# Sparse attention and gated feed-forward in one kernel: the first unit's prologue in another order, block maxima read from PSUM, block means 128 columns wide

## The chip, the cores and the metric

The kernel runs on one core of a Trainium2 chip. A core has five engines with a queue each: TensorE (PE; its weight loads are listed as PEld), VectorE (DVE), ScalarE (ACT), GpSimd (POOL) and SyncE (SP). Here POOL and SP mostly issue transfers. SBUF is the working memory, PSUM the eight banks that TensorE writes. The metric is the device time of one execution in microseconds.

## The reference

Attention over 4 batches, 8 heads, 768 positions and 64 elements a head, in which a query sees its neighbours within 16 positions and one summary for each block of 32 positions: the maximum of the keys and the mean of the values. Its output is the input of a gated feed-forward layer.

```python
k_sum = k.reshape(B, H, nb, block, D).max(axis=3)       # block 32
v_sum = v.reshape(B, H, nb, block, D).mean(axis=3)
mask_l = np.abs(pos[:, None] - pos[None, :]) < window   # window 16
scores_l = np.where(mask_l, scale * q @ k^T, -1e9)
scores_s = scale * q @ k_sum^T + np.log(block)
a = softmax(concat([scores_l, scores_s]))
x = a @ concat([v, v_sum])                              # 3072 x 512
out = x + sigmoid(x @ w_res) * ((gelu(x @ w_gate) * (x @ w_val)) @ w_out)   # 512 -> 1536 -> 512
```

## The kernel before

Inputs are float32; the transfers of k, q, v and the weights turn them into bf16. The work is cut into eight units of 384 positions, two for each batch. Each unit needs attention for its 384 rows, then 12 column blocks of gate and value products (`fo_step`, 4 + 4 products of 128x384 each), then the products with `w_res` and `w_out`. The attention of unit n+1 is laid between the output products of unit n (`first_out`, `mid_out`). Only unit 0 has nothing before it to hide in: its attention is the prologue, lines 476 to 551.

The schedule is manual: each engine's queue holds its instructions in the order in which the code gives them, and an instruction waits for semaphores of the engines that wrote its inputs or last used its buffer. PSUM has four pools: `ps_mm` (four banks, tag mm), `ps_s` (two banks, for a pair's scores), `ps_o` and `ps_t` (one each).

Heads are handled in four pairs. For a pair of unit 0:

- `turn_pair` (L219) transposes the loaded k or q on TensorE into a PSUM tile `tp`.
- `k_place` copies k from PSUM into `kW` with ScalarE (L251). Then VectorE takes the block maxima (`k_blocks`: reduction L236 into `ks`, copy to each tile of 64 queries L240) and copies the neighbours of each tile of 64 keys (`k_rims`, L244 and L245). So each tile's 128 columns are 64 own keys, 32 neighbours, 24 block maxima and 8 unused. `q_place` copies q (ScalarE, L258).
- `s_step` makes the scores: in unit 0 two mask products (L311) write the additive mask, then 12 products (L318) add the scores. ScalarE takes the exponential (L336, or two halves L333 where the scores lie in two separate banks, `MM2`).
- `vsum_pair` makes the block means of v: 12 accumulating products (L284) of a 64x32 averaging matrix `bmat`, out of partitions 96 to 127 of the PSUM tile, copied into `vblk` (L286).
- `pair_rims` copies neighbours of the v tiles (VectorE, L274 and L271). `av_band` multiplies P with the 96 rows of v (L366), `av_blk` with the 32 rows of block means (L366), and `av_end` divides by the sums (L372, L374).
- `xt_step` transposes the result into `xT` (L379, L381), the operand of the gate and value products `gv_mm` (L394). `gv_end` is GELU on ScalarE (L399) and a product on VectorE (L400).

`keep_warm` (L474) is a filler: products of zeros with 512 columns, whose output nobody reads. The first call has 12 of them, before the first k arrives. POOL's queue issues all loads in a fixed order; eight may be under way, and each further one waits for the transfer eight earlier.

## Time and profile before

| what | us |
|---|---|
| median of 4 runs (lowest to highest) | 264.74 (263.96 to 264.91) |
| the profiled execution | 264.91 |
| its span | 263.1 |
| first k arrives, transposes of k start | 6.44 |
| scores of the first pair | 11.08 |
| first attention product | 15.34 |
| first gate product | 26.03 |
| gate product of column block 2 starts | 31.06 |
| TensorE's granted clock is half | 16.12 to 29.77 |

The span is the part of the execution in which the engines have work; the time also counts what lies around it. All places in time are counted from the start of the span. "Idle before" in a row is the engine's gap ahead of an instruction, with what ended it. The granted clock is 1.00 for full speed. It is shown as 1.00 from the start on, but the first 12 fillers run at half speed: 512 columns each 0.42 us, as against 0.22 later. The first change that the trace records is at 5.88.

### The profile page before, as it was taken

The numbers are of one execution on the slowest core, as the hardware profiler recorded it, in microseconds if no ns is written. First come the engines' busy times: TensorE is split into PE (matmuls) and PEld (weight loads), VectorE is DVE, ScalarE is ACT, GpSimd is POOL, SyncE is SP. The second block draws the span as 40 slices with busy tenths as digits, with TensorE's granted clock in tenths as the row PEclk, the third lists the DMA queues.
The fourth block names the chain that finished last, engine by engine and source line by source line (L and its number), as shares of the span: only waits on it lengthen the run. The fifth ranks groups of instructions, "written<-read, shape, count | busy, mean of one in ns | idle before, by whom it ended". The sixth has DMA issues, their size and how long they took to land.

```text
span 263.1 us, 5837 instructions
## 1 busy us (share of the span) xinstructions
PE 253.9 (97%) x2299; PEld 142.6 (54%) x2322; DVE 161.8 (62%) x368; ACT 127.1 (48%) x213; POOL 97.1 (37%) x128
## 2 busy tenths in 40 slices
PE   7889999999999999999999999999999999999994
PEld 2556555456555456545655555545654565556544
DVE  6784289739856744675947744766858544764424
ACT  6754235836666344933373436624383437443320
POOL 8785443540151695029144683238304000000000
PEclk9975799999999999999999999999999999999999
DMA  5999999994901599939932899949903500140003
GB/s 83 169 184 196 197 206 207 165 124 136 145 7 25 127 166 146 124 97 171 120 78 45 140 181 153 99 115 166 150 7 62 161 0 4 35 145 2 2 0 120
DMA packets 98106, 29.33 MB, mean 112 GB/s; under 512 B 83224, under 2 KB 94944, under 8 KB 97984
## 3 DMA queue, kind: packets, MB, share of 16 engines
q0 software_dynamic: 68352, 14.76, 66.7%
q1 hardware_dynamic: 29728, 14.21, 26.3%
q8 instruction: 18, 0.29, 0.5%
q14 instruction: 8, 0.07, 0.1%
HBM read 29.36 MB, written 6.29 MB: 136 GB/s over the span
## 4 chain that ended last, share of the span: by engine, by line
PE 83%; DMA 6%; DVE 6%; issue 2%; POOL 1%; ACT 0%; POOLq 0%; DVEq 0%
PE vv L394 22%; PE g L394 22%; PE f L442 22%; PE r L432 8%; DMA q_sb<-in_q_dram 4%; PE s L318 3%; PE ao L354 3%; DMA k_sb<-in_k_dram 3%; PE tp L219 1%; PE vs L292 1%; DVE vext L556 1%; DVE P L340 1%; DVE ks L236 1%; PE ao L366 1%; DVE o L451 1%
## 5 line engine op out<-in xcount | busy, mean ns | idle before, releaser
L400 DVE TENSOR_TENSOR gvT<-ge,vv 128x384 bf16<-128x384 f32 x96 | 52.7, 553 | 48.7 <-PE vv L394 44.4
L399 ACT ACTIVATE ge<-g 128x384 f32<-128x384 f32 x96 | 47.0, 491 | 71.0 <-DVE gvT L400 38.9
L394 PE MATMUL vv<-xT,w_val 128*128 128x384 bf16 x384 | 79.6, 328 | 0.6 <-DVE gvT L400 0.5
L394 PE MATMUL g<-xT,w_gate 128*128 128x384 bf16 x384 | 79.8, 329 | 0.1
L442 PE MATMUL f<-w_out,gvT 128*128 128x512 bf16 x262 | 62.7, 379 | 1.5 <-issue 1.1
L394 PEld LDWEIGHTS <-w_gate 128*128 128x128 bf16 x384 | 37.4, 99 | 27.1 <-issue 2.6
L394 PEld LDWEIGHTS <-w_val 128*128 128x128 bf16 x384 | 37.8, 98 | 26.2 <-issue 1.7
L442 PEld LDWEIGHTS <-gvT 128*128 128x128 bf16 x276 | 25.7, 98 | 29.5
L107 POOL DMA_DIRECT2D vext<-in_v_dram x32 | 24.5, 793 | 15.4 <-DMA w_out<-in_moe_w_out_dram 5.1
L435 ACT ACTIVATE th<-r 128x512 f32<-128x512 f32 x24 | 13.5, 607 | 27.9 <-PE r L432 27.9
L448 DVE SCALAR_TENSOR_TENSOR th<-th,f 128x512 f32<-128x512 f32 (+2 forms) x26 | 16.6, 640 | 14.6 <-PE f L442 14.6
L432 PE MATMUL r<-w_res,xT 128*128 128x512 bf16 x88 | 22.7, 380 | 0.4
L340 DVE TENSOR_TENSOR P<-P,maskt 128x768 bf16<-128x768 bf16 x28 | 16.7, 597 | 9.9 <-ACT P L336 5.2
L304 POOL COPY vext<-vsum 32x1536 bf16<-32x1536 bf16 x12 | 17.2, 1463 | 13.7 <-DMA vsum<-vpart 13.5
L451 DVE SCALAR_TENSOR_TENSOR o<-th,xn 128x512 f32<-128x512 f32 (+2 forms) x26 | 18.2, 701 | 0.9
L374 DVE TENSOR_TENSOR xn<-ao,rz 128x384 bf16<-128x384 f32 x32 | 17.8, 558 | 1.1
L336 ACT ACTIVATE P<-s,bias_t 128x768 bf16<-128x768 f32 x17 | 15.3, 902 | 6.2 <-PE s L318 6.0
L236 DVE TENSOR_REDUCE ks<-kW 128x24 bf16<-128x768 bf16 x16 | 15.1, 946 | 1.6 <-ACT kW L251 1.6
L127 POOL DMA_DIRECT2D q_nat<-in_q_dram x18 | 15.8, 901 | 0.8 <-issue 0.7
L333 ACT ACTIVATE P<-s,bias_t 128x384 bf16<-128x384 f32 x30 | 15.7, 579 | 0.8 <-PE s L318 0.8
L432 PEld LDWEIGHTS <-xT 128*128 128x128 bf16 x96 | 8.8, 98 | 9.9
L372 DVE RECIPROCAL rz<-ao 128x6 f32<-128x6 f32 x32 | 6.1, 192 | 11.8 <-PE ao L354 9.8
(86 smaller groups left out, 190.1 us busy)
## 6 DMA issues: line engine op xcount, KB each, us to landing
out_dram<-o SPq DMA_DIRECT2D x23, 256.0 KB, 2.2
vext<-in_v_dram POOLq DMA_DIRECT2D x32, 96.0 KB, 6.9
q_nat<-in_q_dram POOLq DMA_DIRECT2D x18, 128.0 KB, 5.5
w_gate<-in_moe_w_gate_dram POOLq DMA_DIRECT2D x6, 256.0 KB, 9.1
w_val<-in_moe_w_val_dram POOLq DMA_DIRECT2D x6, 256.0 KB, 9.7
w_out<-in_moe_w_out_dram POOLq DMA_DIRECT2D x3, 512.0 KB, 14.1
k_nat<-in_k_dram POOLq DMA_DIRECT2D x16, 96.0 KB, 6.0
vext<-vext SPq DMA_DIRECT2D x6, 144.0 KB, 4.8
```

The source lines that it names most:

```text
L107: nc.gpsimd.dma_start(out=vext[b % 2][0:QT, :, h, 0:D], in_=v[b, h].rearrange("(t p) d -> p t d", p=QT))
L236: nc.vector.tensor_reduce(out=ks.rearrange("d (t n) -> d t n", n=2), in_=kw[:, :, 0:QT].rearrange("d t (n w) -> d t n w", w=BLK), axis=myb ...
L304: eng.tensor_copy(vext[b % 2][96:128, lo:hi, :, 0:D], src)
L340: nc.vector.tensor_mul(Pf, Pf, maskt.unsqueeze(1).to_broadcast([128, 2 * HT, QT]))
L374: nc.vector.tensor_mul(xn, ao[:, :, :, 0:D], rz.to_broadcast([128, NSUB, 2, D]))
L394: nc.tensor.matmul(ps[:, 0:TU], w[:, ko, fo * 128:(fo + 1) * 128], st["xT"][:, ko, :], start=(ko == 0), stop=(ko == KO - 1), skip_group_ch ...
L399: nc.scalar.activation(ge[:], g[:, 0:TU], AF.Gelu)
L400: nc.vector.tensor_mul(gvT[:, fo, :], ge[:], vv[:, 0:TU])
L432: nc.tensor.matmul(r[:], st["xT"][:, ko, ss], w_res[:, ko, :], start=(ko == 0), stop=(ko == KO - 1))
L442: nc.tensor.matmul(st["f", sub][:], gvT[:, fo, ss], w_out[:, fo, :], start=(fo == 0), stop=(fo == FO - 1), skip_group_check=True)
L448: nc.vector.scalar_tensor_tensor(th[:, cs], th[:, cs], 1.0, f[:, 0:n], ALU.add, ALU.mult)
L451: nc.vector.scalar_tensor_tensor(o.rearrange("p (k d) -> p k d", d=128), th[:, cs].rearrange("p (k d) -> p k d", d=128), 0.5, x, ALU.mult, ...
```

## The change

The prologue of unit 0 is written in another order, which moves instructions on TensorE, ScalarE and VectorE. All four transposes of the first half (k and q of pairs 0 and 1) come first. Pair 0 then goes to its scores before the second half of k is transposed, and q of pair 1 is placed after the exponential of pair 0. The mask for later units (`maskt`) is made after the last k. The scores of pairs 1 and 2 come before the first attention product, those of pair 3 behind it, and the means of pairs 1 to 3 between the attention products. The fillers are spread otherwise: after the first 12, five, one, one, one and one become one, two, one, one, one and one, some in another bank. The gate and value products of blocks 0 and 1 change their order among each other.

The block maxima of k, where k was transposed on TensorE (batches 0 and 1), are read from the PSUM tile and not from `kW`. The averaging matrix has three zero slots of 32 columns ahead of it, and each block mean product takes four slots as its weights: 128 columns, of which the last 32 are the former ones. The means of pair 3 are copied by ScalarE and no longer by VectorE. The clearing of `bmat` and `bgrp` moves out of `own_keys`.

```diff
-    bmat = const.tile([QT, NT, 32], BF16, name="bmat")
+    bmat = const.tile([QT, NT + 3, 32], BF16, name="bmat")
...
         def own_keys(m, n):
-            nc.vector.memset(m[:], 0.0)
...
-        own_keys(bmat, NT)
+        nc.vector.memset(bmat[:], 0.0)
+        own_keys(bmat[:, 3:, :], NT)
...
-        def k_blocks(b, hp):
+        def k_blocks(b, hp, tp=None):
...
+            if tp is None:
...
+            else:
+                nc.vector.tensor_reduce(
+                    out=ks[:], in_=tp.rearrange("d j (n w) -> d n w j", w=BLK // PJ),
+                    axis=mybir.AxisListType.XY, op=ALU.max)
             nc.vector.tensor_copy(kw[:, :, BAND:BAND + NB], ks.unsqueeze(1).to_broadcast([128, NT, NB]))
...
-        def k_step(b, hp, pool, tag):
-            k_place(b, hp, turn_pair(k_sb[b], hp, turn_tile(k_sb[b], pool, tag)))
+        def k_turn(b, hp, pool, tag):
+            return turn_pair(k_sb[b], hp, turn_tile(k_sb[b], pool, tag))
...
-            k_blocks(b, hp)
+            k_blocks(b, hp, tp)
...
-        def vsum_pair(hp, pool, tag, copy):
+        def vsum_pair(hp, pool, tag):
...
-                nc.tensor.matmul(vs[96:128, 0:2 * D], bmat[:, t, :], vext[0][0:QT, t, hs, 0:D],
+                nc.tensor.matmul(vs[:, 0:2 * D], bmat[:, t:t + 4, :], vext[0][0:QT, t, hs, 0:D],
                                  start=(t == 0), stop=(t == NT - 1))
-            copy(vblk[96:128, hs, 0:D], vs[96:128, 0:2 * D].rearrange("p (h d) -> p h d", d=D))
+            nc.scalar.copy(vblk[96:128, hs, 0:D], vs[96:128, 0:2 * D].rearrange("p (h d) -> p h d", d=D))
...
-        def keep_warm(n):
-            wp = ps_s.tile([128, 2, 512], F32, tag="s", name="wp")
+        def keep_warm(n, pool=ps_s, tag="s"):
+            wp = pool.tile([128, 2 if pool is ps_s else 1, 512], F32, tag=tag, name="wp")
...
-        mm = (ps_mm, "mm")
+        mm, t_bank, o_bank = (ps_mm, "mm"), (ps_t, "t"), (ps_o, "ao")
         keep_warm(12)
-        k_step(0, 0, *mm)
-        k_step(0, 1, *mm)
-        q_step(0, *mm)
-        q_step(1, *mm)
+        tk = {hp: k_turn(0, hp, *mm) for hp in range(2)}
+        tq = {hp: q_turn(hp, *mm) for hp in range(2)}
+        k_place(0, 0, tk[0])
+        q_place(0, 0, tq[0])
+        k_place(0, 1, tk[1])
         mt = ps_o.tile([128, 128], BF16, tag="ao", name="mt")
         nc.tensor.transpose(mt[:], mneg[:], ident[:])
-        nc.vector.tensor_scalar(out=maskt[:], in0=mt[:, 0:QT], scalar1=-1.0, scalar2=None, op0=ALU.is_ge)
-        keep_warm(5)
-        k_step(0, 2, *mm)
-        k_step(0, 3, *mm)
+        keep_warm(1)
         st = new_unit()
         s_step(0, 0, st)
-        s_step(0, 1, st, MM2)
-        t2 = [q_turn(2, *mm), q_turn(3, *mm)]
-        vsum_pair(0, ps_t, "t", nc.scalar.copy)
-        q_place(0, 2, t2[0])
-        q_place(0, 3, t2[1])
-        keep_warm(1)
-        pair_rims(0)
-        vsum_pair(1, ps_o, "ao", nc.scalar.copy)
+        q_place(0, 1, tq[1])
+        keep_warm(2, *t_bank)
+        for hp in range(2, 4):
+            tk[hp] = k_turn(0, hp, *mm)
+            k_place(0, hp, tk[hp])
+        nc.vector.tensor_scalar(out=maskt[:], in0=mt[:, 0:QT], scalar1=-1.0, scalar2=None, op0=ALU.is_ge)
+        for hp in range(2, 4):
+            tq[hp] = q_turn(hp, *mm)
+            q_place(0, hp, tq[hp])
+        s_step(0, 1, st)
+        keep_warm(1, *t_bank)
+        vsum_pair(0, *t_bank)
+        s_step(0, 2, st, MM2)
...
+        pair_rims(0)
+        av_band(0)
+        s_step(0, 3, st)
         pair_rims(1)
-        av_band(0)
         av_blk(0)
-        s_step(0, 2, st)
+        vsum_pair(1, *o_bank)
+        pair_rims(2)
         av_band(1)
-        s_step(0, 3, st, MM2)
-        pair_rims(2)
         av_blk(1)
-        vsum_pair(2, ps_t, "t", nc.scalar.copy)
+        vsum_pair(2, *t_bank)
         nc.scalar.activation(gate1[:], bias_t[0:1, :], AF.Gelu)
         keep_warm(1)
+        pair_rims(3)
         av_band(2)
-        pair_rims(3)
-        vsum_pair(3, ps_o, "ao", nc.vector.tensor_copy)
...
         av_blk(2)
-        xt_step(0, 0, st, **turn[0])
+        keep_warm(1)
...
+        xt_step(0, 0, st, **t_turn)
+        vsum_pair(3, *o_bank)
         av_band(3)
+        xt_step(0, 1, st, **t_turn)
         keep_warm(1)
         av_blk(3)
-        xt_step(0, 1, st, **turn[1])
-        keep_warm(1)
...
```

The rest of the diff is the new order of the gate and value products of blocks 0 and 1 with the last two transposes between them: g0 (0, 1), transpose 2, g1 (0, 1), g0 (2), g1 (2), transpose 3, v0 (0 to 2), v1 (0 to 2), then the last part of each.

## The prediction

> **What bounds the kernel now.** I read the page first: the span, the engines, and the row of the TensorE clock.

> ```profile
> span 263.1 us, 5837 instructions
> ...
> PE 253.9 (97%) x2299; PEld 142.6 (54%) x2322; DVE 161.8 (62%) x368; ACT 127.1 (48%) x213; POOL 97.1 (37%) x128
> ...
> PEclk9975799999999999999999999999999999999999
> ```

> TensorE is busy 97% of the span, but between slices 2 and 4 its granted clock is not full. I then cut that stretch finer. The columns are: stretch, its length, busy time and instructions of PE, PEld, DVE, ACT, POOL, then granted clock, DMA share, GB/s.

> ```profile
> 5.88:9.29 3.41, 2.97 (x55) 1.59 (x54) 2.01 (x21) 2.27 (x4) 3.14 (x5) 1.00 1.30 189
> 9.29:12.71 3.42, 2.87 (x80) 2.00 (x80) 3.07 (x10) 2.29 (x4) 2.31 (x4) 1.00 2.17 157
> 12.71:16.12 3.41, 2.59 (x50) 1.90 (x48) 3.25 (x11) 2.34 (x7) 3.20 (x5) 1.00 2.21 167
> 16.12:19.53 3.41, 3.41 (x56) 2.02 (x55) 2.54 (x7) 1.66 (x3) 2.85 (x5) 0.50 1.46 197
> 22.95:26.36 3.41, 3.41 (x47) 2.12 (x47) 1.81 (x5) 0.96 (x2) 2.24 (x3) 0.50 1.45 196
> 26.36:29.77 3.41, 3.41 (x16) 1.99 (x15) 0.36 (x1) 0.48 (x1) 1.85 (x3) 0.50 1.45 196
> 29.77:33.19 3.42, 3.33 (x21) 1.87 (x20) 1.57 (x3) 1.36 (x3) 1.61 (x3) 1.00 1.46 200
> ```

> The clock is halved from 16.12 to 29.77, 13.65 us, and TensorE has no idle time in it: this is where the prologue can win. Up to 15.34 other engines set the pace. The timeline of these engines, then of TensorE:

> ```profile
> 10.42 1.50 ACT L251 COPY kW<-tp 128x768 bf16<-128x768 bf16 x2 [1.14 <-PE tp L219]
> 11.25 0.95 DVE L236 TENSOR_REDUCE ks<-kW 128x24 bf16<-128x768 bf16 x1 [0.28 <-ACT kW L251]
> 14.82 0.46 DVE L271 COPY vext<-vext 16x768 bf16<-16x768 bf16 x1
> ```

> ```profile
> 15.34 0.38 PE L366 MATMUL ao<-vext,P 96*64 96x65 bf16 x12 [0.43 <-DVE vext L271]
> ...
> 19.13 1.46 PE L284 MATMUL vs<-vext,bmat 64*32 64x128 bf16 x12
> ...
> 26.03 0.53 PE L394 MATMUL g<-xT,w_gate 128*128 128x384 bf16 x1
> ...
> 31.06 0.81 PE L394 MATMUL g<-xT,w_gate 128*128 128x384 bf16 x4
> ```

> The first attention product waits for the V rims that VectorE ends at 15.29. The chain of waits then names a transfer:

> ```profile
> 19.20 1.40 PE vs L284 x12
> 20.61 0.48 issue
> 21.08 9.96 DMA q_sb<-in_q_dram
> 31.04 0.01 issue
> 31.06 0.81 PE g L394 x4
> ```

> I don't believe it: TensorE has no gap there, and the tile is read only at 42.85. My mark is the start of the third gate product, 31.06; from there on the two kernels run the same order.

> [...] here a window with TensorE busy 2.59 of 3.41 us was followed by the drop, and three with no idle time did not end it[...]. [...] No reduction from PSUM is in this trace.

> **The change part by part**, against the profiled 264.91 us (span 263.1, 1.8 around it; the median of the runs is 264.74, 0.17 less).

> *Block maxima from PSUM.* The built program shows each reduction still waiting for ScalarE's copy of the same pair, so it starts no earlier. 0.946 us now; [...] I take 0. It holds its PSUM bank longer: the q transpose of pair 2 waits for the second reduction, which ends at 10.15, before its own data. The four reductions of batch 1 change too; their banks' next users come a product block (1.3 us) or more later.

> *Block means 128 wide.* Twelve products take 0.84 us at full clock and 1.46 at half (spacing 54 and 107 ns), which is their 128 moving columns. The weight load grows from 56 ns to the 98 of other 128-wide loads; 128-wide ones of half the rows keep up at 12 in 0.35 us (the scores). I take 0, at worst 12 x 44 ns x 4 = 2.1 us if a load no longer overlaps. The gain is that each fills half the array, not an eighth.

> *New order, to the first attention product.* Pair 0 goes first: its copy 7.01-7.82, reduction 7.84-8.79, rims to 9.30, scores to 9.65 (now 11.4), exponential (0.9) to 10.57. It now stands ahead of q 1 (0.44) and of the K copy of pair 2, so that starts at 11.0, not 10.42. Behind it: reduction 11.82-12.77, rims to 13.25, last reduction and rims to 14.75, mask 0.17, V rims of pair 0 (0.83) to 15.85. So the attention product of pair 0 starts 0.5 us LATER, and TensorE, done with the scores of pair 2 by 14.15, idles 1.7 us. For this, scores of pairs 1 and 2 lie before it; ScalarE's row (copies to 12.5, q to 13.4, exponentials 0.9 + 1.05, one means copy) ends at 15.6, and the last exponential at 17.8, not 19.8.

> *From 15.85 on at full clock.* Attention band 0.31, last scores 0.7, rest of pair 0 0.31 (17.15); means 1, 0.68 (17.85); pair 1 with its means copy 0.26 between, 0.65 (18.5); means 2 and a filler (19.4); pair 2, a filler, transpose (20.5); means 3 (21.1). VectorE's V rims and normalizations (0.83 and 0.76 each) end at 20.5 for pair 3, before it. Band 3 (21.4); the second transpose waits for the first's copy out of the same bank, which waits for ScalarE's table load (19.5-21.0): 21.75. Filler, rest of pair 3 (22.25); then 16 gate and value products at 0.163 with two transposes and their copies: 25.6. That is 5.4 us before 31.06. I take off 0.5, about 0.03 for each of some 16 hand-overs between engines (the chain shows 0.02 to 0.05): **-4.9 us**.

> *Moved past queues.* POOL's transfers keep their order and are released by the transfer eight earlier, so they land where they land now. Read from these releases: gate chunk 1 by 21.1 (used 31.06), q half 1 by 32.7 (42.85), w_res 37.9 (46.9), w_out 40.5 to 45.5 (49.4 to 54.6), k of batch 1 49.3 (61.3). The least cover is 9 us; it hides a shift of 5. SP's queue starts later and keeps its order. The changed memset grows from 64x192 to 64x240 words, 0.05 us under the wait for k. Between 31 and 43 VectorE's fill-in work sets the pace now and then (idle before gate products 0.50 at the most); it is the same work and moves with the rest.

> **The clock decides.** I count moving columns times the used share of rows and of weight columns; a full window at 0.163 us per 384 is 8,040. Before the drop (12.71-16.12): 22 means x 16, one filler 512, attention 391, mask product about 400: 1,655, 21%. The window before, which kept the clock: mask 1,536, scores 768, transposes 1,728, means 64: 51%, or 29% without transposes. So the bar is between 21% and 29 or 51. The changed kernel there: 11 means x 64, mask 768, scores 384, two thirds of a band 195: 2,051, 25%. From 16.12 it has 40% and more. That is inside the bracket; I take it as just enough, because the means alone go from 352 to 704 columns. With whole columns counted instead of cells, it is 39% against 29% at the drop.

> **Rivals.** *The same drop.* The 1.7 us of idle time leaves the window too thin, and the clock halves at 16.12 as now. Then TensorE's own work is the bound: at 16.12 the new order still has means 1 (1.40) and the rest of pair 0 (0.52) to do, the old one most of one score block (1.0): 0.9 us more, of which half is run after 29.77 at double speed: +0.45, 265.4.

> *Slower: an earlier drop.* Fillers before 9.29 go from five to one. In 5.88-9.29 I count fillers 1,024, mask 896, transposes 1,728: 45%, as against 58% now; but without transposes 24% against 35%. If transposes don't count and the bar is above 24%, the clock halves at 9.29. The next window's transposes, scores and means at half speed cost 1.35 more; the first gate product starts at 28.4 instead of 26.03. If the window to 29.77 still counts as full, the end is +1.1 us, 266.0; if not, all 16 products run at 0.325 until 33.19: +2.8, 267.7.

> *Part of the gain.* The clock holds at 16.12 but falls for one window later, or wide loads don't overlap: 2 to 3 us lost, 262.5. *It doesn't do what it says*: true of the reductions, above; it costs nothing.

> **How the numbers follow.** Full clock 52% (own range 258.4 to 261.5), part 8%, same drop 23%, earlier drop 17%. The likeliest gives 264.91 - 4.9 = 260.0. The range runs from 258.4 to 266.0, over the two middle cases and the near half of the earlier drop. 0.3% (0.8 us) is about what a measurement can tell. Faster: 52 + 7 = 59%. Within 0.3%: two thirds of the same drop and 1, 16%. Slower: the rest of it and the earlier drop, 25%.

> **What would show it.** Right: clock 1.00 in every window after the first start, scores of pair 0 near 9.3, the first attention product near 15.85, gate products of the third column block near 26, and the shift carried unchanged to the end. Wrong: a clock of 0.50 from about 16 (same drop) or 9.3 (earlier), a K copy of pair 2 that starts before 10.6, means spaced wider than 60 ns, or TensorE waiting for a weight transfer.

## The result, and the profile after

The changed kernel takes 265.27 us (median of 12 runs, 263.94 to 266.19); the kernel before took 264.09 beside it (median of 17 runs, 258.88 to 265.08). The difference of the medians is +1.18 us, 0.4% slower; the prediction was 260.0. The ratio of the comparison is 1.0201, 95% interval 1.0144 to 1.0257, but it sets the mean of all 12 runs against that of before's four fastest alone (258.88, 258.93, 259.46 and 262.75).

That spread belongs to the result. In the profiles, an execution at a mean clock of 0.998 to 1.0 has no half-clock stretch in its course, one at 0.980 (e9) has one of some 10.2 us, one at 0.972 or 0.973 (before, after) has one of 13.65 us: three and four windows of 3.41 us. Over this comparison and those of the experiments, before was under 260 us in 14 of 65 runs. The changed kernel never was: four runs at 0.980 (263.94 to 264.36), eight at 0.972 to 0.974 (264.79 to 266.19). Where before's clocks are listed (48 runs, those beside the experiments), its medians are 259.22 at the full clock (11 runs), 263.47 at 0.980 (21) and 264.84 below 0.975 (16); the changed kernel's are 264.27 and 265.97. So it is 0.8 to 1.1 us slower at a like clock, and none of its runs has the full clock, which one run of before in five has. Twelve runs without one could come by chance, about one time in eighteen; e10 and e14 below, which leave the gap open or fill it with few rows, add eight more without one.

The page of the profile after (265.39 us, the span 1.9 less), its span, engines and granted clock:

```profile
span 263.5 us, 5834 instructions
...
PE 253.5 (96%) x2296; PEld 142.9 (54%) x2320; DVE 159.9 (61%) x367; ACT 127.1 (48%) x213; POOL 96.8 (37%) x128
...
PEclk9985699999999999999999999999999999999999
```

The stretch cut at the steps of the clock (columns as in the prediction: stretch, length, busy time and instructions of PE, PEld, DVE, ACT, POOL, clock, DMA share, GB/s):

```profile
6.93:10.35 3.42, 2.54 (x59) 1.48 (x54) 2.27 (x5) 2.30 (x4) 2.55 (x4) 1.00 1.43 186
10.35:13.76 3.41, 3.35 (x78) 2.41 (x77) 2.27 (x9) 3.41 (x7) 2.85 (x5) 1.00 2.43 158
13.76:17.17 3.41, 1.71 (x52) 1.05 (x50) 2.74 (x9) 1.82 (x5) 3.25 (x5) 1.00 1.81 177
17.17:20.59 3.42, 3.42 (x58) 3.02 (x51) 2.38 (x7) 1.06 (x2) 2.46 (x4) 0.50 1.48 201
20.59:24.00 3.41, 3.41 (x41) 2.17 (x40) 1.42 (x4) 2.23 (x4) 1.66 (x3) 0.50 1.43 192
24.00:27.41 3.41, 3.05 (x40) 2.23 (x40) 0.72 (x2) 0.74 (x2) 2.10 (x3) 0.50 1.45 196
27.41:30.83 3.42, 3.42 (x16) 1.76 (x15) 0.39 (x2) 0.48 (x1) 1.75 (x3) 0.50 1.45 197
30.83:34.24 3.41, 3.32 (x21) 1.92 (x20) 1.73 (x4) 1.59 (x4) 1.57 (x3) 1.00 1.39 202
```

The clock is half for four windows again, from 17.17 to 30.83 (before 16.12 to 29.77). The window that the drop follows has TensorE busy for 1.71 of 3.41 us; before it was 2.59. The timeline of VectorE, then of ScalarE:

```profile
11.93 0.96 DVE L242 TENSOR_REDUCE ks<-tp 128x24 bf16<-128x768 bf16 x1 [1.07 <-ACT kW L256]
15.52 0.36 DVE L273 COPY vext<-vext 16x768 bf16<-16x768 bf16 x1
```

```profile
11.09 1.51 ACT L256 COPY kW<-tp 128x768 bf16<-128x768 bf16 x2
```

And TensorE:

```profile
12.70 0.83 PE L286 MATMUL vs<-vext,bmat 64*128 64x128 bf16 x12
...
15.94 0.38 PE L368 MATMUL ao<-vext,P 96*64 96x65 bf16 x12 [1.70 <-DVE vext L273]
...
17.30 1.46 PE L286 MATMUL vs<-vext,bmat 64*128 64x128 bf16 x12
...
26.54 0.82 PE L396 MATMUL g<-xT,w_gate 128*128 128x384 bf16 x2
...
31.87 0.81 PE L396 MATMUL g<-xT,w_gate 128*128 128x384 bf16 x4
```

What the first attention product waits for comes as forecast, to a tenth: a K copy of pair 2 at 11.09 (11.0 foretold), V rims ready at 15.88 (15.85), and ahead of the first attention product a gap of 1.70 us (1.7). Then twelve means take 1.46 us, not 0.84. The gate product of column block 2 starts at 31.87, 0.81 later than before, where 4.9 earlier was foretold. The chain of waits, in the same stretch, no longer names a transfer of q:

```profile
17.36 1.39 PE vs L286 x12
...
29.37 1.76 PE vv L396 x6
```

From 17.2 to 30.8 TensorE's own work at half clock is the path. The two kernels run the same order from there on, and 0.48 us of the shift are left in the executions' times (265.39 against 264.91). So the order of work came out as planned, and the clock did not hold.

### The profile page after: what moved, and what is told of

The parts are those of the page before. It is cut to its first block, busy times and chain, and to the rows that moved or that the text cites. A ratio compares the mean times of both kernels' runs of the same rounds, so it can differ in the third digit from the quotient of the medians.

```text
span 263.5 us, 5834 instructions
## 1 busy us (share of the span) xinstructions
PE 253.5 (96%) x2296; PEld 142.9 (54%) x2320; DVE 159.9 (61%) x367; ACT 127.1 (48%) x213; POOL 96.8 (37%) x128
## 4 chain that ended last, share of the span: by engine, by line
PE 90%; DVE 5%; issue 2%; ACT 1%; DVEq 0%
PE g L396 23%; PE vv L396 23%; PE f L444 23%; PE r L434 8%; PE ao L356 3%; PE s L320 3%; PE wp L476 2%; PE vs L286 2%; PE ao L368 1%; PE tp L219 1%; DVE ks L242 1%; PE vs L294 1%; PE xp L381 1%; DVE vext L558 1%; DVE o L453 1%
## 5 line engine op out<-in xcount | busy, mean ns | idle before, releaser
L107 POOL DMA_DIRECT2D vext<-in_v_dram x32 | 24.1, 784 | 15.5 <-DMA w_out<-in_moe_w_out_dram 5.4
L450 DVE SCALAR_TENSOR_TENSOR th<-th,f 128x512 f32<-128x512 f32 (+2 forms) x26 | 16.6, 640 | 14.4 <-PE f L444 14.4
L306 POOL COPY vext<-vsum 32x1536 bf16<-32x1536 bf16 x12 | 17.2, 1463 | 10.5 <-DMA vsum<-vpart 10.4
L338 ACT ACTIVATE P<-s,bias_t 128x768 bf16<-128x768 f32 x18 | 16.3, 904 | 6.6 <-PE s L320 6.4
L376 DVE TENSOR_TENSOR xn<-ao,rz 128x384 bf16<-128x384 f32 x32 | 17.8, 558 | 1.1
L335 ACT ACTIVATE P<-s,bias_t 128x384 bf16<-128x384 f32 x28 | 14.6, 577 | 0.0
L121 POOL DMA_DIRECT2D k_nat<-in_k_dram x16 | 12.1, 800 | 0.6 <-issue 0.6
```

The costliest lines, as they stand in the source:

```text
L107: nc.gpsimd.dma_start(out=vext[b % 2][0:QT, :, h, 0:D], in_=v[b, h].rearrange("(t p) d -> p t d", p=QT))
L306: eng.tensor_copy(vext[b % 2][96:128, lo:hi, :, 0:D], src)
L338: nc.scalar.activation(P.rearrange("p a t q -> p a (t q)"), s2[:, :, 0:TU], AF.Exp, scale=scale, bias=bias_t[:])
L376: nc.vector.tensor_mul(xn, ao[:, :, :, 0:D], rz.to_broadcast([128, NSUB, 2, D]))
L450: nc.vector.scalar_tensor_tensor(th[:, cs], th[:, cs], 1.0, f[:, 0:n], ALU.add, ALU.mult)
```

## The experiments

My theory from here: the gap of 1.70 us, left empty, costs the clock. First rival: the width of the products sets it, as the prediction had it. Second rival: the clock falls whatever is done there. Times beside an experiment are of before on the same chip.

### The gap filled (e1, e2, e3)

Each adds fillers after the scores of pair 2 (`s_step(0, 2, ...)`), where TensorE waits for the V rims anyway.

e1 uses full fillers, e2 seven of 64 rows x 32 columns, e3 28 transposes of 128x128.

```diff
         s_step(0, 2, st, MM2)
+        keep_warm(7)
```

```diff
         s_step(0, 2, st, MM2)
+        wn = ps_s.tile([128, 2, 512], F32, tag="s", name="wn")
+        for _ in range(7):
+            nc.tensor.matmul(wn[0:32, 0], warm[0:64, 0:32], warm[0:64], start=True, stop=True)
```

```diff
         s_step(0, 2, st, MM2)
+        wn = ps_s.tile([128, 2, 1024], BF16, tag="s", name="wn")
+        for i in range(28):
+            nc.tensor.transpose(wn[:, 0, (i % 4) * 128:(i % 4) * 128 + 128], warm[:, 0:128], ident[:])
```

> The changed kernel with seven 128-wide fillers (512 columns, 0.216 us each at full clock) in the 1.70 us in which TensorE waits for the V rims before the first attention product; nothing else is changed. Theory A (the clock falls because too little of the array works in that window): the window's share rises from about 23% to some 65%, the clock stays 1.00 beyond 17.17 us, the third gate product starts near 26 instead of 31.87, and the time is about 260 us. Rival B (the half clock comes whatever TensorE does there, after three full windows): 0.50 again from 16 to 17.5 us, and 265 us. Rival C (the clock is held over this window, but the next ones, with 40 to 55%, let it fall): 262 to 264 us, the fall one or two windows of 3.41 us later.

> As the filled gap, but the seven fillers use 64 rows and 32 weight columns, an eighth of the array, with the same 512 moving columns and the same 1.5 us of TensorE time. If the clock follows the busy TIME of TensorE: as good as the wide fillers, about 260 us. If it follows the SHARE of the array that works (theory A): the window goes only from 23% to 29%, the clock falls as in the changed kernel, and the time is 265 us.

> As the filled gap, but with 28 transposes of 128x128 (54 ns each, 1.5 us) in place of the seven fillers. If transposes count like products: about 260 us, as with the wide fillers. If they do not count for the clock: it falls, 265 us. This also says which of the two counts (with or without transposes) bounds the bar.

Measured: e1 260.46 us (259.89 to 262.96), e2 259.89 (259.85 to 260.83), e3 260.23 (260.20 to 260.48); before 264.50. Twelve of the 13 runs have a clock of 0.998 to 1.0; one of e1 has 0.984 and 262.96. The timeline of TensorE in e2:

```profile
14.03 1.68 PE L505 MATMUL wn<-warm 64*32 64x512 bf16 x7
15.91 0.38 PE L368 MATMUL ao<-vext,P 96*64 96x65 bf16 x12 [0.20 <-DVE vext L273]
...
26.42 0.81 PE L396 MATMUL g<-xT,w_gate 128*128 128x384 bf16 x4
```

The attention product starts where it did (15.91 against 15.94): the fillers cost nothing there and bring some 5 us. Left empty, this gap costs the clock. And fillers that use an eighth of the array do it as well as full ones (e2: 0.998 to 1.0 in all four runs): the share of the array isn't the measure. Transposes do it too (e3: the same in all four).

### Half of the gap, another place, two short gaps (e9, e10, e11)

e9 puts three fillers in the gap; e10 leaves the gap open and puts three more ahead of the scores of pair 0; e11 has no filler more, but makes VectorE copy the V rims of pair 0 before it works on K of pair 3.

```diff
         s_step(0, 2, st, MM2)
+        keep_warm(3)
```

```diff
-        keep_warm(1)
+        keep_warm(4)
         st = new_unit()
         s_step(0, 0, st)
```

```diff
             tk[hp] = k_turn(0, hp, *mm)
+            if hp == 3:
+                pair_rims(0)
             k_place(0, hp, tk[hp])
...
-        pair_rims(0)
         av_band(0)
```

> The changed kernel with three fillers of 128x512 in the gap ahead of the first attention product in place of the seven of the first experiment: 3 x 0.213 = 0.64 us of the 1.70 us are filled, and 1.06 us of idle stay. If the dose counts (a certain occupied share of one clock window is wanted), the result falls between: some runs at the full clock (259.9 to 260.5) and some at 263.9 to 266.2. If any cover of the gap will do, all runs are at 259.9 to 260.5; if only a gap of about the 0.2 us of the first experiments keeps the clock, all are at 263.9 to 266.2.

> The changed kernel with four fillers in place of one ahead of the scores of head pair 0 (7.9 us in the trace), where TensorE waits 0.45 us for K; the gap of 1.70 us ahead of the first attention product is left open. If that gap is what costs the clock: 263.9 to 266.2, no run at a mean clock of 1.0, and the clock falls between 15 and 18 us of the span. If the lean stretch from 7 to 12 us costs it (the rival of the prediction with an earlier drop), the fill mends it: 259.9 to 260.9 at a clock of 1.0.

> The changed kernel without any filler more, but with VectorE's two rim copies of V for head pair 0 moved ahead of its work on K of head pair 3. The first attention product should start at about 14.4 in place of 15.94, with an idle time of about 0.3 us ahead of it, and the scores of head pair 3 then wait about 0.7 us for their keys: one gap of 1.7 us becomes two short ones with 0.4 us of products between. If one long gap is what costs the clock: 259.4 to 260.0, all runs at 1.0. If the occupied share of a window counts: about 1 us of idle stays in the same window, so part or all of the runs stay at 263.5 to 266. If neither gap nor window counts: 264.9, which is the changed kernel less the 0.4 us by which the scores of head pair 3 come earlier.

Measured, before 263.38: e9 263.73 (259.91 to 264.11), one run of four at 1.0 and three at 0.980. e10 265.13 (264.00 to 266.88), none of four at 1.0; in its profile the clock falls at about 15.3, while the gap (14.30 to 16.11) is still open. e11 262.78 (259.09 to 264.94): of 19 runs five at 1.0 (259.09 to 259.39), five at 0.987, five at 0.978 to 0.980, four at 0.973 or 0.974. TensorE in e9, in e10, and in e11:

```profile
13.98 0.81 PE L476 MATMUL wp<-warm 128*128 128x512 bf16 x3
15.81 0.38 PE L368 MATMUL ao<-vext,P 96*64 96x65 bf16 x12 [1.02 <-DVE vext L273]
```

```profile
16.11 0.54 PE L368 MATMUL ao<-vext,P 96*64 96x65 bf16 x12 [1.81 <-DVE vext L273]
```

```profile
14.17 0.38 PE L368 MATMUL ao<-vext,P 96*64 96x65 bf16 x12
14.48 0.50 PE L313 MATMUL s<-ident,mneg 128*128 128x384 bf16 x2
15.55 0.20 PE L320 MATMUL s<-qT,kW 64*128 64x64 bf16 x2 [0.57 <-DVE kW L249]
```

So the dose counts: 1.5 us of filler kept the clock in 12 of the 13 runs of e1 to e3, 0.64 us in one run of four, and without any filler in the gap none of the changed kernel's twelve runs kept it. The early fillers change nothing that four runs show, and the changed kernel's own profile has the full clock until 17.17, so the prediction's rival with an earlier drop is not what happened. e11 removes the long gap without any filler, and the clock still falls in 14 of 19 runs. So the case of "one long gap" is out, and the other one of the expectation, which looks at a whole window, fits: in these runs it isn't one gap but what TensorE does over a longer time. In e11's profile the drop comes at about 19.0, after the short gaps and a run of means and attention products.

### Rows or columns (e13, e14)

What of the work counts? Both fill the gap with seven products of 512 columns, 0.213 us each, on a quarter of the array: one tall and narrow, one flat and wide.

e13, 128 rows x 32 columns:

```diff
         s_step(0, 2, st, MM2)
+        wn = ps_s.tile([128, 2, 512], F32, tag="s", name="wn")
+        for _ in range(7):
+            nc.tensor.matmul(wn[0:32, 0], warm[:, 0:32], warm[:], start=True, stop=True)
```

e14, 32 rows x 128 columns:

```diff
         s_step(0, 2, st, MM2)
+        wn = ps_s.tile([128, 2, 512], F32, tag="s", name="wn")
+        for _ in range(7):
+            nc.tensor.matmul(wn[:, 0], warm[0:32, 0:128], warm[0:32], start=True, stop=True)
```

> The changed kernel with seven fillers in the gap that use 128 rows x 32 columns of the array and stream 512 columns each: 7 x 0.213 = 1.5 us, as before, at a quarter of the array. If occupied time counts: 259.8 to 260.9 at a clock of 0.998 to 1.0, as with 64 x 32. If the rows fed count: the same. If the columns in use count: part or all of the runs at 263.5 to 266.

> The changed kernel with seven fillers in the gap that use 32 rows x 128 columns, the same duration and the same quarter of the array. If occupied time counts: 259.8 to 260.9 at a clock of 0.998 to 1.0. If the rows fed count (in the traces so far, the share of the 128 rows that TensorE is fed in a window of 3.41 us, read 0.5 us ahead of its end, was up to 0.46 where the clock fell and 0.45 or more where it stayed): the gap adds only 0.11 to that share, and most runs are at 262 to 266.

Measured, before 264.24: e13 260.61 (259.68 to 260.79), clock 0.998 to 1.0 in all four runs; e14 265.42 (263.14 to 265.65), clock 0.972 to 0.987, none of four at 1.0. TensorE in e13, then in e14, then e14 by windows:

```profile
14.39 1.69 PE L505 MATMUL wn<-warm 128*32 128x512 bf16 x7
16.27 0.38 PE L368 MATMUL ao<-vext,P 96*64 96x65 bf16 x12 [0.20 <-DVE vext L273]
```

```profile
14.25 1.68 PE L505 MATMUL wn<-warm 32*128 32x512 bf16 x7
16.13 0.38 PE L368 MATMUL ao<-vext,P 96*64 96x65 bf16 x12 [0.20 <-DVE vext L273]
16.44 0.82 PE L313 MATMUL s<-ident,mneg 128*128 128x384 bf16 x2
```

```profile
13.02:16.43 3.41, 3.21 (x44) 1.70 (x41) 3.28 (x10) 2.22 (x5) 3.41 (x5) 1.00 2.08 171
16.43:19.84 3.41, 3.41 (x55) 2.43 (x50) 2.55 (x6) 1.15 (x2) 2.90 (x5) 0.50 1.44 196
```

The durations are the same (1.69 and 1.68), and so are the gap that is left (0.20) and the share of the array. In e14 TensorE is busy for 3.21 of 3.41 us, 94%, and the clock falls right after: the mask products at 16.44 take 0.82 in place of 0.50. So neither occupied time nor the share of the array decides in these two runs; how many of the 128 rows the operands fill does. In these products the weights and the moving operand fill the same rows, so the runs do not tell which of the two counts. With 512 columns each, seven fillers add, of the 8,040 columns that fit into 3.41 us at 0.163 us per 384, 45% in e13 (and in e1), 22% in e2 and 11% in e14. Those that add 22% or more keep the clock (12 of the 13 runs of e1, e2 and e13 at 0.998 to 1.0); e14 doesn't (none of four), although it uses more of the array than e2.

Counted afterwards, over the profiles of before, after and the 15 experiments: for every product its columns times its share of rows, as a share of those 8,040, in the 3.41 us that end 0.5 us ahead of each place where the clock stepped or, whole multiples of 3.41 us from such a step, could have stepped. The windows ahead of a drop hold 0.32 (after), 0.33 (e11), 0.34 (e14), 0.39 (e4), 0.40 (e9), 0.41 (before), 0.44 (e10), 0.46 (e1, e7). Those that kept the clock hold 0.42 (once, e15), 0.45 (e8), 0.46 (e6, e15), and 0.47 or more. The two sets overlap between 0.42 and 0.46. The half microsecond is chosen so that this fits best, so it describes these profiles and is not a rule that was tested; that rows might decide, and what e14 would then show, was written down before e13 and e14 ran.

### The widths of the means, and the maxima (e4, e7, e8)

e4 is the kernel before with only the means made 128 wide (and `bmat` three slots longer for it); e7 is the changed kernel with e1's fillers and the means 32 wide again; e8 is the same with the maxima taken from `kW` again.

```diff
...
-                nc.tensor.matmul(vs[96:128, 0:2 * D], bmat[:, t, :], vext[0][0:QT, t, hs, 0:D],
+                nc.tensor.matmul(vs[:, 0:2 * D], bmat[:, t:t + 4, :], vext[0][0:QT, t, hs, 0:D],
```

```diff
-                nc.tensor.matmul(vs[:, 0:2 * D], bmat[:, t:t + 4, :], vext[0][0:QT, t, hs, 0:D],
+                nc.tensor.matmul(vs[96:128, 0:2 * D], bmat[:, t + 3, :], vext[0][0:QT, t, hs, 0:D],
...
```

```diff
-            k_blocks(b, hp, tp)
+            k_blocks(b, hp)
...
```

> The kernel before, with one part of the change alone: the block mean products 128 columns wide (and the memsets that go with it). At equal clock it costs nothing: spacing 54 ns as before, the first attention product at 15.3 us. The share in the window before the drop goes from 21% to about 34%. If the bar lies under that, the clock holds and the time falls to about 259 us more often than before; if it lies above, 264 us as before. If wide weight loads don't overlap, each group of twelve takes up to 0.5 us more.

> The changed kernel with the gap filled, the block mean products 32 columns wide again. At full clock the spacing is 54 ns either way: 260 us. If width counts for the clock, the clock falls in more runs than with wide means (one of five there): 262 to 265 us in most runs; if only busy time counts, as the narrow fillers said: no more than there.

> The changed kernel with the gap filled, the block maxima read from the copied K in SBUF again. The reduction takes 0.945 us either way and waits for the same copy: no difference, 260 us. A reading from PSUM that pays would show as 0.1 us or more of loss here.

Measured: e4 263.06 (259.12 to 263.44; before 264.50), one run of four at 1.0, three at 0.980. Before itself mixes in that way, so e4 alone is inconclusive. e7 260.85 (260.02 to 262.83), three of four at 0.999 or 1.0, as e1: 32-wide means keep the clock about as often, which agrees with rows, 64 either way. e8 259.93 (259.74 to 260.47). A reduction from SBUF in e8, on VectorE's timeline:

```profile
11.70 0.95 DVE L237 TENSOR_REDUCE ks<-kW 128x24 bf16<-128x768 bf16 x1 [0.80 <-ACT kW L256]
```

It takes 0.95 us against 0.96 from PSUM, and waits for the same copy. Neither part of the change moves the time by what these runs can tell.

### The old order with fillers (e5)

```diff
         q_place(0, 3, t2[1])
-        keep_warm(1)
+        keep_warm(2)
         pair_rims(0)
         vsum_pair(1, ps_o, "ao", nc.scalar.copy)
+        keep_warm(2)
```

> The kernel before with three more fillers, which no longer leave TensorE idle ahead of its first attention product (0.38 us from 13.69, 0.44 us from 14.90): two in place of one after the q copies of pairs 2 and 3, and two after the means of pair 1. If busy time decides the clock: the clock holds in most runs, the time is 259 us, 5 us under the median of before, and about 1 us under the changed kernel with its gap filled (259.9). If it is chance that the clock holds: half of the runs or fewer at 259 us. If the order of the changed kernel is the faster one at equal clock: over 260 us.

Measured: 259.48 (259.36 to 259.93), all four runs at 0.999 or 1.0; before 263.42 (259.22 to 264.54). TensorE:

```profile
15.83 0.38 PE L366 MATMUL ao<-vext,P 96*64 96x65 bf16 x12 [0.67 <-DVE vext L271]
...
25.95 0.81 PE L394 MATMUL g<-xT,w_gate 128*128 128x384 bf16 x4
```

Three fillers in the old order bring the time that the whole reordering was meant to reach. By the medians this version is 3.9 us faster than before beside it. It takes what before's own two runs at the full clock beside it take, 259.22 and 259.70: the fillers add no speed, they keep the clock.

### What is left of the new order at full clock (e6, e12, e15)

With fillers the new order takes 259.9 to 260.5, the old one 259.5, on different chips; before's own runs at the full clock lie between 258.72 and 259.70 over all chips. Three tries to find the half microsecond. e6 puts the K copies of pairs 2 and 3 and q of pair 1 ahead of the scores of pair 0; e12 undoes the order of means, attention and transposes behind pair 2; e15 is e11 with three fillers in the second short gap. e6 and e12 have e1's fillers.

```diff
-        st = new_unit()
-        s_step(0, 0, st)
         q_place(0, 1, tq[1])
         keep_warm(2, *t_bank)
         for hp in range(2, 4):
             tk[hp] = k_turn(0, hp, *mm)
             k_place(0, hp, tk[hp])
+        st = new_unit()
+        s_step(0, 0, st)
```

```diff
-        pair_rims(3)
         av_band(2)
+        pair_rims(3)
+        vsum_pair(3, *o_bank)
...
         av_blk(2)
-        keep_warm(1)
         xt_step(0, 0, st, **t_turn)
-        vsum_pair(3, *o_bank)
         av_band(3)
-        xt_step(0, 1, st, **t_turn)
         keep_warm(1)
         av_blk(3)
+        xt_step(0, 1, st, **o_turn)
+        keep_warm(1)
```

```diff
         av_band(0)
+        keep_warm(3)
         s_step(0, 3, st)
```

> The changed kernel with the gap filled, and one part of the new order undone: the K copies of pairs 2 and 3 (with their transposes) and the q copy of pair 1 go ahead of the scores and the exponential of pair 0 again. If the late K copy of pair 2 is what the new order loses at equal clock: that copy starts near 10.5, the first attention product near 15.3 to 15.5 instead of 15.9 to 16.2, and 0.5 us less than the filled changed kernel, 259.4 us. If the loss lies behind the first attention product (the second transpose that waits for the table load and the first's copy): 260 us as before.

> The changed kernel with the seven fillers of the first experiment, and with the order of the kernel before from the band product of head pair 2 to the last transposes (mean of V for pair 3 ahead of the block product of pair 2, the second transposes into the other bank and after the block product of pair 3); the order of the gate and value products stays the changed one. If this order is why the filled new order is slower than the filled old one (259.9 to 260.5 against 259.5): 259.4 to 259.7, and the wait of 0.24 us for the copy of xT at 24.05 is gone. If the loss is not there: 259.9 to 260.5.

> The changed kernel with the rim copies of V for head pair 0 moved ahead of the work on K of head pair 3, and three fillers of 128x512 (0.64 us) in the 0.8 us that the scores of head pair 3 then wait for their keys. If the two short gaps are what still cost the clock in 14 of 19 runs of the version without fillers: all runs at a clock of 1.0 and at 259.1 to 259.5, as the five undisturbed ones there, and faster than the old order with fillers (259.36 to 259.93). If the stretch behind (block products 32 rows deep) costs it: some runs at a clock of 0.987 and 262.

Measured: e6 261.54 (261.15 to 263.64; before 263.42), e12 260.76 (260.63 to 260.81; before 263.38), e15 260.09 (259.75 to 261.95, one of four at 0.984; before 264.24). All three miss the time; of e15, one run fell as its second case had it. TensorE in e6:

```profile
13.13 0.48 PE L313 MATMUL s<-ident,mneg 128*128 128x384 bf16 x2 [0.88 <-ACT P L338]
...
15.75 1.68 PE L476 MATMUL wp<-warm 128*128 128x512 bf16 x7
17.36 0.38 PE L368 MATMUL ao<-vext,P 96*64 96x65 bf16 x12
```

The scores of pair 1 wait there for the exponential of pair 0, which holds their PSUM tile, and the fillers now stand in the way: the V rims are ready at 15.75, and the attention product starts at 17.36. So e6 says nothing about the K copies. In e12 the values of v landed 0.9 us later in the profiled run than in e2 (means at 13.46 against 12.56), but from the first attention product to the gate product of block 2 it also took longer, 10.85 us against 10.51, where e5 takes 10.12. So undoing the order of that stretch did not win it back, and where the 0.4 us between 10.51 and 10.12 goes stays open. In e15 the attention product waits for ScalarE's P until 14.84 (14.17 in e11), the fillers run behind it from 15.15, and the scores of pair 3 come at 16.45 (15.55 to 15.98 in e11): what the earlier rims had won is gone.

## Why the prediction was wrong

- *Block maxima from PSUM*: right. 0.94 to 0.96 us from either place, behind the same copy (e8). *It doesn't do what it says* was true and cost nothing.
- *Block means 128 wide*: right on the cost, since twelve took 0.83 us at full clock and 1.46 at half. Wrong on the gain: "each fills half the array, not an eighth" shows no worth to the clock (e7).
- *New order, to the first attention product*: right, 15.94 against 15.85, with the idle time of 1.7 us found in advance.
- *From 15.85 on at full clock*: nearly right. With the clock held, the gate product of block 2 starts at 26.42 in e2 (25.6 plus 0.5 foretold, 26.1) and the kernel takes 259.89; the forecast of 260.0 is the time of the changed kernel with its gap filled. But before takes 259.22 where its own clock holds, so all of the 4.9 us was the clock's, and the order itself brings none of it.
- *Moved past queues*: agrees. No transfer shows on the path behind 17 us.
- *The clock decides* is the step that failed, in "I take it as just enough". The sum counted rows times weight columns: 21% for the window before the drop in before, 25% for the changed kernel. The trace gives about 25% for the window that the drop follows, so the figure was right and the measure wrong. That the used share of the array sets the clock was my assumption; the trace of before shows neither this nor the contrary. In the runs, of the two factors only the rows go with the clock (e13 against e14, e2). The same sum with rows alone: before, means 22 x 64 = 1,408, filler 512, attention 780, mask about 400, together 3,100, 39%; changed, means 11 x 64 = 704, mask 768, scores 384, two thirds of a band 390, together 2,246, 28%. Counted so, the changed kernel is fed less than the one whose clock already fell. The prediction's cross-check, 39% against 29%, kept the columns and dropped the rows, the wrong one of the two. The widening of the means, from 352 to 704 in my sum, was the whole of its lead, and by rows it adds nothing.
- A second fault lies under it. The 1.7 us of idle time was in the forecast, and I let a bracket (21% to 29 or 51) from one execution outvote it. The kernel before was near the edge: 14 of its 65 runs keep the clock. Its single profile and its four times shown, 263.96 to 264.91, tell nothing of that: all four lie among the times of runs with three or four windows at half clock. And the steps of the clock do not lie at the same places in every execution: the first that the trace records comes at 5.88 us in before and at 6.93 in after, and the stretches at half clock last 6.8 us (e11), 10.2 (e9) or 13.65 (before, after), all multiples of 3.41. I laid the changed kernel's work into the windows of before's execution: its drop came at 17.17, not 16.12.
- *The same drop* is what happened. It foretold +0.45 us to 265.4; the profiled executions differ by 0.48 (265.39 against 264.91), the medians by 1.18, as before's also count its runs at the full clock; at a like clock the change costs 0.8 to 1.1. That the profiles agree so closely is in part luck, since the drop came 1.05 us later than this case had it.

## What to carry to other kernels

The stage in which TensorE waits for other engines was priced twice here: by the wait (1.70 us), and by the clock of what followed (0.50 for 13.65 us). Before a reorder is judged by its path, look at how TensorE is fed in every stretch of the length that the clock's steps show (3.41 us here), counting (in this kernel) the rows of the operands and not how wide or how busy a product is, and try fillers over all 128 rows where it waits anyway (e1: 260.46 us in place of 265.27). Where the times of one kernel fall into groups some microseconds apart, compare the groups by the granted clock, and take more than one profile before saying what a kernel does.
